# A fused layer norm, state-space and gated feed-forward kernel: the first transposed tile split over two PSUM banks and two copy engines, the second tile in a third bank, end waits sorted

## Chip, cores and metric

The kernel runs on one core of one Trainium2 chip. The metric is device microseconds of one execution on that core. Before the change it took 179.96 us (median of 3 executions, 179.96 to 180.11).

The change touches some half a microsecond of a 180 us kernel.

## The reference

The input x is 2048 rows of 512 numbers in bf16. It is normalised once, and two branches are added to it. Cut to what matters:

```
xn  = layernorm(x)                                     # over the 512 columns
# branch A: a diagonal complex state space with 512 states
h_t = Lam_bar * h_(t-1) + B_bar @ xn_t                 # scan over the 2048 rows
A   = 2 * real(h @ C.T) + xn * Dskip                   # Lam_bar = exp(exp(log_dt) * Lambda)
# branch B: gated feed-forward, 1376 hidden columns
Bf  = (gelu(xn @ w_gate) * (xn @ w_up)) @ w_down
out = x + A + Bf
```

## The kernel before

The rows are worked in four blocks of 512, each of four tiles of 128 rows. The kernel's matmuls take the normalised x with its 512 columns on the partitions, so each tile is transposed. In the first block TensorE does that: four transposes of 128x128 write one PSUM bank, and one engine copies the bank to SBUF.

```
def TR0(j, eng):                       # tile j of the first block
    if not TBANK:
        TBANK.extend([next_bank(), next_bank()])
    bank = TBANK[j % 2]
    ...
    PE(f, ...)                         # four transposes, one instruction group, into this bank
    dst = XNT[0].ap[:, :, 128 * j:128 * (j + 1)]
    src = pt[:, 0:512].rearrange("p (q t) -> p q t", q=KD)
    if eng == "A":
        GATE["evTA"] = ACT(lambda e: e.activation(dst, src, ACTF.Copy), ...)     # ScalarE copies
    else:
        GATE["evT"] = V(lambda e: e.tensor_copy(dst, src), ...)                  # VectorE copies
```

The start of the program, with what TensorE does in this order:

```
PE(fwarm, ...)                         # 11 matmuls on constants, the warm-up
LN(0, [0, 1], True)                    # layer norm of tiles 0 and 1
TR0(0, "V")                            # tile 0: transposes, VectorE copies
TR0(1, "A")                            # tile 1: transposes, ScalarE copies
fill(2)                                # two more matmuls on constants
LN(0, [2, 3], True, [GATE["evT"]])     # tiles 2, 3: statistics only after a VectorE copy
load_B()                               # more loads: the second and third batch of x, B, weights
GU_first(range(5), range(3))           # gate and up projections of the first block
...
```

The first 12 matmuls in `GU_first` are gate projections of tile 0 (three column groups of 128, four matmuls each). The next 12 are up-projections of tile 0 and need the first chunk of `w_up`, a load issued at the start:

```
for u in range(2):                     # 0: gate, 1: up
    for ft in early:                   # three column groups
        mm(ft, u, 0, 1)                # 4 matmuls, tile 0 only
params()                               # one transpose of parameters, and small VectorE/GpSimd work
for ft in early:
    for u in range(2):
        mm(ft, u, 1, 2)                # tile 1
late = [ft for ft in fts if ft not in early]
mm(late[0], 0, 0, 2)
TR0(2, "V")                            # tiles 2 and 3
TR0(3, "A")
...
```

TensorE and the load queue keep the order of the program text, but VectorE, ScalarE and GpSimd are ordered by a list scheduler in the kernel, from estimated durations. So an edit of the first microseconds can reorder VectorE anywhere. And the layer norms of later blocks compute the square root of the variance as a power on GpSimd (line L609 below; VectorE then takes the reciprocal).

```
def SKIP(b):
    ...
        V(lambda e, ...: e.tensor_tensor(XD[tt].ap, xs.ap, DSKB.ap, ALU.mult), ...)      # L621
```

At the very end the queue that issues the stores waits for every output store:

```
final_waits = [(op.sem, 16) for op in self.out_ops]
```

Of the kernel before, what the change touches and what calls it, by code (L numbers as in the profile page):

```python
# [10 lines left out]
ACTF = mybir.ActivationFunctionType  # L11
BF16, F32, I32 = dt.bfloat16, dt.float32, dt.int32
# [64 lines left out]
class Sched:  # L77
# [205 lines left out]
    def emit(self):  # L283
        nc, es = self.nc, self.es
        order = self.order
        esem = {}
        for e in ENGINES:
            if any(op.kind == "eng" for op in order[e]):
                esem[e] = es.enter_context(nc.semaphore("q_" + e))
        cnt = {e: 0 for e in ENGINES}  # L290
        nd = 0
        for e in ENGINES:
            for op in order[e]:
                if op.kind == "eng":
                    cnt[e] += 1
                    op.sem, op.val = esem[e], cnt[e]
                else:
                    op.sem, op.val = es.enter_context(nc.semaphore("d%d" % nd)), 16
                    nd += 1
        self.n_sems = len(esem) + nd  # L300
        plan = {}
        nwait = 0
        for e in ENGINES:
            seen = {}
            prog = []
            for op in order[e]:
                need = {}
                for d in op.deps:
                    if d.kind == "eng" and d.eng == e and e == "tensor":
                        continue  # L310
                    key = ("e", d.eng) if d.kind == "eng" else ("d", d.id)
                    if seen.get(key, 0) >= d.val:
                        continue
                    if key not in need or need[key].val < d.val:
                        need[key] = d
                for key, d in need.items():
                    seen[key] = d.val
                waits = [(d.sem, d.val) for d in need.values()]
                nwait += len(waits)
                prog.append((waits, op))  # L320
            plan[e] = prog
        self.n_waits = nwait
        final_waits = [(op.sem, 16) for op in self.out_ops]
        block = es.enter_context(nc.Block())

        def body_for(ename):
            prog = plan[ename]

            def body(h):
                for waits, op in prog:  # L330
                    for (s, v) in waits:
                        h.wait_ge(s, v)
                    ins = op.fn(h)
                    ins.then_inc(op.sem, 1 if op.kind == "eng" else 16)
                if ename == "sync":
                    for (s, v) in final_waits:
                        h.wait_ge(s, v)
            return body

        for e in ENGINES:  # L340
            if plan[e] or e == "sync":
                {"tensor": block.tensor, "vector": block.vector, "scalar": block.scalar,
                 "gpsimd": block.gpsimd, "sync": block.sync}[e](body_for(e))
# [3 lines left out]
NT, NB, KD, KP, KF = 16, 4, 4, 4, 11  # L347
# [6 lines left out]
def d_pe(n_list):  # L354
    return sum(n / 2.4 + 2.5 for n in n_list)
# [5 lines left out]
def d_act(n, ptr=0): return 190.0 + 0.833 * n + 90.0 * ptr  # L361
# [3 lines left out]
def build(nc, ins, out):  # L365
    with ExitStack() as es:
# [4 lines left out]
        A = Arena(arena_t, ARENA_BYTES)  # L371
        PS = [E(nc.psum_tensor("PS%d" % i, [128, 512], F32)) for i in range(8)]
        BANK = [Buf("bank%d" % i, "ps", i, i + 1) for i in range(8)]

        def ring(parent, name, n):
            return [A.sub(parent, "%s%d" % (name, i), i) for i in range(n)]
# [11 lines left out]
        XNT = ring(XNT_all, "XNT", NB)  # L388
# [3 lines left out]
        XN = ring(XN_all, "XN", 8)  # L392
        DSKB = A.alloc("DSKB", [D], BF16)
        XD_all = A.alloc("XD", [NT, D], BF16); XD = ring(XD_all, "XD", NT)
        IDN = A.alloc("IDN", [128], BF16)
# [20 lines left out]
        XT0 = XTk[0]  # L416
# [88 lines left out]
        V = lambda fn, dur, r, w, tag="", after=(): S.op("vector", fn, dur, r, w, tag, after)  # L505
        ACT = lambda fn, dur, r, w, tag="", after=(): S.op("scalar", fn, dur, r, w, tag, after)
        POOL = lambda fn, dur, r, w, tag="": S.op("gpsimd", fn, dur, r, w, tag)
        PE = lambda fn, dur, r, w, tag="": S.op("tensor", fn, dur, r, w, tag)
# [14 lines left out]
        def next_bank():  # L523
            b_ = rstate["n"] % 8
            rstate["n"] += 1
            return b_
# [24 lines left out]
        GATE = {"before_gelu": [], "nh": 0}  # L551
# [71 lines left out]

        TBANK = []

        def TR0(j, eng):
            if not TBANK:
                TBANK.extend([next_bank(), next_bank()])
            bank = TBANK[j % 2]
            pt = PS[bank].bitcast(BF16)  # L630

            def f(e):
                ins_ = None
                for q in range(KD):
                    ins_ = e.transpose(pt[:, 128 * q:128 * (q + 1)], XN[j].ap[:, 128 * q:128 * (q + 1)], IDN.ap)  # L635
                return ins_
            PE(f, 56.0 * KD, [XN[j], IDN], [BANK[bank]], "T0")
            dst = XNT[0].ap[:, :, 128 * j:128 * (j + 1)]
            src = pt[:, 0:512].rearrange("p (q t) -> p q t", q=KD)
            if eng == "A":  # L640
                GATE["evTA"] = ACT(lambda e: e.activation(dst, src, ACTF.Copy), d_act(512), [BANK[bank]], [XT0[j]], "evT")
            else:
                GATE["evT"] = V(lambda e: e.tensor_copy(dst, src), 420, [BANK[bank]], [XT0[j]], "evT")  # L643

        def TR(b):
            tts = list(range(4 * b, 4 * b + 4))
# [62 lines left out]
            V(lambda e: e.tensor_tensor(ssb.ap[:, :, 1, :], TB.ap[:, :, 0, :], TA.ap[:, :, 1, :], ALU.subtract),  # L709
              d_dve_tt2x(2048), [TA, TB], [SSc[k3][s][1] for s in range(KP)], "post_im")  # L710

        def GU_first(fts, early):
            banks = [{ft: next_bank() for ft in fts} for h in range(2)]

            def mm(ft, u, j0, j1):
                W, Wc = ((WG, WGc), (WU, WUc))[u]
                h, q0 = j0 // 2, 256 * u + 128 * (j0 % 2)
                bank = banks[h][ft]

                def f(e):  # L720
                    ins_ = None
                    for dk in range(KD):
                        ins_ = e.matmul(PS[bank][:, q0:q0 + 128 * (j1 - j0)], W.ap[:, dk, 128 * ft:128 * (ft + 1)],  # L723
                                        XNT[0].ap[:, dk, 128 * j0:128 * j1], start=(dk == 0), stop=(dk == KD - 1))
                    return ins_
                PE(f, d_pe([128 * (j1 - j0)] * 4), [Wc[wchunk(ft)]] + XT0[j0:j1], [BANK[bank]], "GU0")

            def evac(ft, h, after=()):
                bank, c0 = banks[h][ft], 256 * h
                GATE["nh"] = kk = (GATE["nh"] + 1) % 3  # L730
                GATE["last_gelu"] = ACT(lambda e: e.activation(GG[kk].ap[:, 0:256], PS[bank][:, 0:256], ACTF.Gelu_apprx_tanh),
                                        d_act(256), [BANK[bank]], [GG[kk]], "gelu", after)
                ACT(lambda e: e.activation(UPB[kk].ap[:, 0:256], PS[bank][:, 256:512], ACTF.Copy),
                    d_act(256), [BANK[bank]], [UPB[kk]], "evU")
                V(lambda e: e.tensor_tensor(HTt[0][ft].ap[:, c0:c0 + 256], GG[kk].ap[:, 0:256], UPB[kk].ap[:, 0:256], ALU.mult),
                  d_dve_tt2x(256), [GG[kk], UPB[kk]], [HTt[0][ft]], "hmul")

            for u in range(2):
                for ft in early:
                    mm(ft, u, 0, 1)  # L740
            params()
            for ft in early:
                for u in range(2):
                    mm(ft, u, 1, 2)
            late = [ft for ft in fts if ft not in early]
            mm(late[0], 0, 0, 2)
            TR0(2, "V")
            TR0(3, "A")
            for ft in early:
                evac(ft, 0, [GATE["evTA"]])  # L750
            for ft in late[1:]:
                mm(ft, 0, 0, 2)
            for ft in late:
                mm(ft, 1, 0, 2)
                evac(ft, 0)
            for ft in fts:
                for u in range(2):
                    mm(ft, u, 2, 4)
                evac(ft, 1)
# [123 lines left out]
        def fill(n):  # L883
            def f(e):
                ins_ = None
                for _ in range(n):
                    ins_ = e.matmul(PS[wb][:, 0:128], WRM.ap, WRM.ap, start=True, stop=True)
                return ins_
            PE(f, 60.0 * n, [WRM], [BANK[wb]], "fill")

        PE(fwarm, d_pe([512] * nwarm) * 1.6, [WRM], [BANK[wb]], "warm")
        LN(0, [0, 1], True)
        TR0(0, "V")
        TR0(1, "A")
        fill(2)
        LN(0, [2, 3], True, [GATE["evT"]])
        load_B()
        GU_first(range(5), range(3))
        tables_dve()
        GATE["before_gelu"] = [tables_act([GATE["last_gelu"]])]  # L900
        BU(0)
# [81 lines left out]
```

## Time and profile before

| | before |
|---|---|
| time, median of 3 | 179.96 us |
| profiled execution | 179.44 us, span 177.6 us |
| TensorE busy | 97% of the span |
| chain of waits on TensorE | 95% |

The first two lines of the page, and its part 4, the shares of the chain of waits that ended last. Busy is in us, then the share of the span and the number of instructions; PE is TensorE, DVE is VectorE, ACT is ScalarE, POOL is GpSimd.

```profile
span 177.6 us, 2519 instructions
...
PE 172.8 (97%) x914; PEld 86.6 (49%) x929; DVE 156.5 (88%) x276; ACT 91.9 (52%) x175; POOL 11.0 (6%) x20
...
PE 95%; DVE 2%; DMA 1%; issue 1%; ACT 0%; DVEq 0%; ACTq 0%
```

TensorE, with 97% of the span and 95% of the chain, is the bottleneck. VectorE is busy for 88% of the span, but has 2% of the chain. The chain of waits of the kernel before, in order of time, shows where TensorE is not yet the limit. Columns: start in us, length in us, what.

```profile
5.20 0.42 DVE arena L614
...
5.67 0.41 PE PS L635 x4
6.08 0.02 issue
6.10 0.43 DVE arena L643
6.54 0.14 issue
6.67 1.50 PE PS L723 x24
...
10.16 0.45 PE PS L635 x8
10.61 5.68 PE PS L723 x52
```

L614 is the normalisation of tile 0, L635 the transposes, L643 VectorE's copy, L723 the gate and up matmuls. Up to 6.67 us the chain runs through the load, the layer norm and the copy. After that it is TensorE with steps of 0.05 us between. So the change works on the last 0.57 us before TensorE takes over: the copy and the hand-over after it.

The timeline of the kernel before in that stretch: start, length, engine, line, operation, and in brackets how long the engine had been idle and who released it. Copies, transposes and matmuls of one group are merged into one line.

```profile
6.10 0.42 DVE L643 COPY arena<-PS 128x512 bf16<-128x512 bf16 x1 [0.17 <-PE PS L635]
...
6.43 0.60 ACT L641 ACTIVATE arena<-PS 128x512 bf16<-128x512 bf16 x1 [1.54 <-PE PS L635]
6.63 1.29 DVE L602 BATCH_NORM_STATS2 arena<-arena 128x6 f32<-128x512 bf16 x2
```

VectorE takes 0.42 us for tile 0. ScalarE takes 0.60 us for the same size of tile 1. VectorE begins the statistics of tiles 2 and 3 (L602) at 6.63.

### The profile page before, as it was taken

The numbers are of one execution on the slowest core, as the hardware profiler recorded it, in microseconds if no ns is written. First come the engines' busy times: TensorE is split into PE (matmuls) and PEld (weight loads), VectorE is DVE, ScalarE is ACT, GpSimd is POOL, SyncE is SP. The second block draws the span as 40 slices with busy tenths as digits, with TensorE's granted clock in tenths as the row PEclk, the third lists the DMA queues.
The fourth block names the chain that finished last, engine by engine and source line by source line (L and its number), as shares of the span: only waits on it lengthen the run. The fifth ranks groups of instructions, "written<-read, shape, count | busy, mean of one in ns | idle before, by whom it ended". The sixth has DMA issues, their size and how long they took to land.

```text
span 177.6 us, 2519 instructions
## 1 busy us (share of the span) xinstructions
PE 172.8 (97%) x914; PEld 86.6 (49%) x929; DVE 156.5 (88%) x276; ACT 91.9 (52%) x175; POOL 11.0 (6%) x20
## 2 busy tenths in 40 slices
PE   7899999999999999999999999999999999999994
PEld 2697464444644444444644444444464444444453
DVE  5759997999998999789999999899999999999211
ACT  3289998976766899002577495000677800900000
POOL 3110028000000002400000000000000000000000
PEclk9999999999999999999999999999999999999999
DMA  5999914988045000002024000000001000003011
GB/s 135 332 302 174 316 28 91 200 222 285 0 95 56 0 0 0 2 30 92 0 59 89 0 6 0 30 30 30 30 4 30 0 0 0 0 0 122 30 51 37
DMA packets 26387, 12.90 MB, mean 73 GB/s; under 512 B 17704, under 2 KB 26376, under 8 KB 26376
## 3 DMA queue, kind: packets, MB, share of 16 engines
q1 hardware_dynamic: 25824, 12.36, 28.4%
q10 hardware_dynamic: 552, 0.40, 0.9%
q8 instruction: 7, 0.11, 0.3%
q14 instruction: 4, 0.03, 0.0%
HBM read 6.46 MB, written 2.10 MB: 48 GB/s over the span
## 4 chain that ended last, share of the span: by engine, by line
PE 95%; DVE 2%; DMA 1%; issue 1%; ACT 0%; DVEq 0%; ACTq 0%
PE PS L838 37%; PE PS L798 34%; PE PS L660 15%; PE PS L723 5%; PE PS L772 3%; DMA arena<-in_A_x_dram 1%; DVE arena L602 1%; PE PS L635 0%; DVE arena L643 0%; DVE arena L614 0%; DVE arena L856 0%; DVE arena L603 0%; ACT arena L607 0%; DVE arena L605 0%; DVE arena L610 0%
## 5 line engine op out<-in xcount | busy, mean ns | idle before, releaser
L838 PE MATMUL PS<-arena 128*128 128x512 bf16 (+3 forms) x317 | 65.9, 366 | 0.3
L798 PE MATMUL PS<-arena 128*128 128x512 bf16 x273 | 60.7, 379 | 0.4
L838 PEld LDWEIGHTS PS<-arena 128*128 128x128 bf16 (+1 forms) x323 | 30.8, 98 | 35.2
L813 ACT ACTIVATE arena<-PS 128x512 bf16<-128x512 f32 x35 | 20.9, 599 | 43.4 <-PE PS L798 32.8
L798 PEld LDWEIGHTS PS<-arena 128*128 128x128 bf16 x280 | 27.3, 98 | 32.1
L693 DVE TENSOR_TENSOR_SCAN arena<-arena 128x512 bf16<-128x512 f32 x32 | 38.8, 1252 | 0.0
L660 PE MATMUL PS<-arena 128*128 128x512 bf16 x126 | 28.0, 379 | 0.1
L816 ACT ACTIVATE arena<-PS 128x512 bf16<-128x512 f32 x35 | 20.8, 598 | 5.6 <-PE PS L798 5.4
L856 DVE TENSOR_TENSOR arena<-PS,arena 128x512 bf16<-128x512 f32 (+2 forms) x17 | 10.9, 651 | 10.4 <-PE PS L838 10.4
L660 PEld LDWEIGHTS PS<-arena 128*128 128x128 bf16 x128 | 12.5, 98 | 14.9
L664 ACT ACTIVATE arena<-PS 128x512 bf16<-128x512 f32 x32 | 17.8, 603 | 3.2 <-PE PS L660 3.2
L818 DVE TENSOR_TENSOR arena<-arena 128x512 bf16<-128x512 bf16 x35 | 14.0, 416 | 1.5 <-ACT arena L816 1.2
L830 ACT ACTIVATE PS<-arena 128x512 f32<-128x512 bf16 (+2 forms) x17 | 9.6, 581 | 6.1 <-DVE arena L856 5.5
L602 DVE BATCH_NORM_STATS2 arena<-arena 128x6 f32<-128x512 bf16 x16 | 10.3, 682 | 1.6 <-DMA arena<-in_A_x_dram 1.5
L723 PE MATMUL PS<-arena 128*128 128x256 bf16 (+1 forms) x104 | 9.3, 248 | 0.2 <-DVE arena L643 0.2
L680 DVE TENSOR_TENSOR arena<-arena 128x4096 bf16<-128x4096 bf16 (+1 forms) x5 | 9.3, 1856 | 0.0
L682 DVE TENSOR_TENSOR arena<-arena 128x4096 bf16<-128x4096 bf16 (+1 forms) x5 | 9.3, 1855 | 0.0
L706 DVE TENSOR_TENSOR arena<-arena 128x4096 bf16<-128x4096 bf16 x4 | 9.1, 2284 | 0.0
L705 DVE TENSOR_TENSOR arena<-arena 128x4096 bf16<-128x4096 bf16 x4 | 9.1, 2283 | 0.0
L723 PEld LDWEIGHTS PS<-arena 128*128 128x128 bf16 x104 | 8.1, 98 | 0.9 <-issue 0.3
L614 DVE TENSOR_SCALAR arena<-arena 128x512 bf16<-128x512 bf16 x16 | 5.7, 405 | 0.3
L772 PE MATMUL PS<-arena 128*128 128x192 bf16 x64 | 5.9, 246 | 0.0
(86 smaller groups left out, 107.7 us busy)
## 6 DMA issues: line engine op xcount, KB each, us to landing
out_dram<-arena SPq DMA_DIRECT2D x15, 128.0 KB, 1.7
arena<-in_A_x_dram SPq DMA_DIRECT2D x3, 512.0 KB, 7.2
arena<-in_B_w_down_dram SPq DMA_DIRECT2D x1, 1280.0 KB, 6.9
arena<-in_A_x_dram SPq DMA_DIRECT2D x4, 128.0 KB, 2.9
arena<-in_B_w_gate_dram SPq DMA_DIRECT2D x1, 512.0 KB, 6.1
arena<-in_B_w_up_dram SPq DMA_DIRECT2D x1, 512.0 KB, 7.0
arena<-in_B_w_gate_dram SPq DMA_DIRECT2D x1, 480.0 KB, 4.1
arena<-in_B_w_up_dram SPq DMA_DIRECT2D x1, 480.0 KB, 5.2
```

The source lines that it names most:

```text
L602: V(lambda e, tt=tt: e.bn_stats(ST[tt].ap, X[tt].ap), d_dve_1x(512), [X[tt]], [ST[tt]], "bnst", after)
L660: ins_ = e.matmul(PS[bank][:, :], BBT[c][dk].ap[:, 128 * s:128 * (s + 1)], XNT[b].ap[:, dk, :], start=(dk == 0), stop=(dk == KD - 1))
L664: ACT(lambda e, bank=bank, k3=k3, s=s, c=c: e.activation(SSc[k3][s][c].ap, PS[bank][:, :], ACTF.Copy), d_act(512), [BANK[bank]], [SSc[k3][ ...
L693: V(lambda e, g=g, rb=rb, init=init: e.tensor_tensor_scan(g.ap, rb, g.ap, init, ALU.mult, ALU.add), d_dve_scan(512), [g, PA[RRr]] + ([CARc ...
L723: ins_ = e.matmul(PS[bank][:, q0:q0 + 128 * (j1 - j0)], W.ap[:, dk, 128 * ft:128 * (ft + 1)], XNT[0].ap[:, dk, 128 * j0:128 * j1], start=( ...
L772: ins_ = e.matmul(dst, XNT[b].ap[:, dk, 128 * j:128 * (j + 1)], WGU[:, :, dk, f0:f0 + m], start=(dk == 0), stop=(dk == KD - 1))
L798: ins_ = e.matmul(PS[bank][0:m, c0:c1], W.ap[:, dk, 128 * ft:128 * ft + m], XNT[b].ap[:, dk, c0:c1], start=(dk == 0), stop=(dk == KD - 1))
L813: GATE["last_gelu"] = ACT(lambda e, bg=bg, kk=kk, m=m: e.activation(GG[kk].ap[0:m, :], PS[bg][0:m, :], ACTF.Gelu_apprx_tanh), d_act(512), ...
L816: ACT(lambda e, bu=bu, kk=kk, m=m: e.activation(UPB[kk].ap[0:m, :], PS[bu][0:m, :], ACTF.Copy), d_act(512), [BANK[bu]], [UPB[kk]], "evU")
L818: V(lambda e, kk=kk, m=m, ft=ft, k2=k2: e.tensor_tensor(HTt[k2][ft].ap[0:m, :], GG[kk].ap[0:m, :], UPB[kk].ap[0:m, :], ALU.mult), d_dve_tt ...
L838: ins_ = e.matmul(PS[bank][:, c0:c1], l_[:, 128 * j:128 * (j + 1)], r_[:, c0:c1], start=False, stop=last and n == len(ops) - 1, skip_group ...
L856: V(lambda e: e.tensor_tensor(OUTB[ko].ap[:, c0:c1], PS[bank][:, c0:c1], XD[tt].ap[:, c0:c1], ALU.add), d_dve_1x(c1 - c0), [BANK[bank], XD ...
```

## The change

The intent: tile 0 should reach SBUF earlier when two engines each copy half of it. The halves go to different PSUM banks. Tile 1 then goes to a third bank (one that the gate and up projections use later), so that in the program it waits for no copy of tile 0. VectorE copies it in place of ScalarE. Sorting the end waits by the modelled landing time is to save a little at the end. The two filler matmuls are dropped. The core of the diff:

```diff
-        final_waits = [(op.sem, 16) for op in self.out_ops]
+        final_waits = [(op.sem, 16) for op in sorted(self.out_ops, key=lambda o: o.finish)]
...
-        def TR0(j, eng):
+        def TR0(j, engs, first=None):
...
+            per = KD // len(engs)
+            toks = [XT0[j]] if len(engs) == 1 else [Buf("XT0_%d_%d" % (j, n), ...) for n in range(len(engs))]
+            for n, eng in enumerate(engs):
+                bank = TBANK[(j + n) % 2] if first is None else first
...
+                    for q in range(per):
+                        k = per * n + q
+                        ins_ = e.transpose(pt[:, 128 * q:128 * (q + 1)], XN[j].ap[:, 128 * k:128 * (k + 1)], IDN.ap)
...
+                dst = XNT[0].ap[:, per * n:per * (n + 1), 128 * j:128 * (j + 1)]
...
-        TR0(0, "V")
-        TR0(1, "A")
-        fill(2)
+        TR0(0, "VA")
+        hbanks = [{ft: next_bank() for ft in range(5)} for h in range(2)]
+        TR0(1, "V", hbanks[0][4])
         LN(0, [2, 3], True, [GATE["evT"]])
         load_B()
-        GU_first(range(5), range(3))
+        GU_first(range(5), range(3), hbanks)
```

More of the change, by code (lines that the diff above doesn't have):

```diff
@@ L624, in build, with f @@
         TBANK = []
-        def TR0(j, eng):
+        def TR0(j, engs, first=None):
             if not TBANK:
                 TBANK.extend([next_bank(), next_bank()])
-            bank = TBANK[j % 2]
-            pt = PS[bank].bitcast(BF16)
-            def f(e):
-                ins_ = None
-                for q in range(KD):
-                    ins_ = e.transpose(pt[:, 128 * q:128 * (q + 1)], XN[j].ap[:, 128 * q:128 * (q + 1)], IDN.ap)
-                return ins_
-            PE(f, 56.0 * KD, [XN[j], IDN], [BANK[bank]], "T0")
-            dst = XNT[0].ap[:, :, 128 * j:128 * (j + 1)]
-            src = pt[:, 0:512].rearrange("p (q t) -> p q t", q=KD)
-            if eng == "A":
-                GATE["evTA"] = ACT(lambda e: e.activation(dst, src, ACTF.Copy), d_act(512), [BANK[bank]], [XT0[j]], "evT")
-            else:
-                GATE["evT"] = V(lambda e: e.tensor_copy(dst, src), 420, [BANK[bank]], [XT0[j]], "evT")
+            per = KD // len(engs)
+            toks = [XT0[j]] if len(engs) == 1 else [Buf("XT0_%d_%d" % (j, n), "xt", j + n / len(engs), j + (n + 1) / len(engs))
+                                                    for n in range(len(engs))]
+            for n, eng in enumerate(engs):
+                bank = TBANK[(j + n) % 2] if first is None else first
+                pt = PS[bank].bitcast(BF16)
+                def f(e, n=n, pt=pt):
+                    ins_ = None
+                    for q in range(per):
+                        k = per * n + q
+                        ins_ = e.transpose(pt[:, 128 * q:128 * (q + 1)], XN[j].ap[:, 128 * k:128 * (k + 1)], IDN.ap)
+                    return ins_
+                PE(f, 56.0 * per, [XN[j], IDN], [BANK[bank]], "T0")
+                dst = XNT[0].ap[:, per * n:per * (n + 1), 128 * j:128 * (j + 1)]
+                src = pt[:, 0:128 * per].rearrange("p (q t) -> p q t", q=per)
+                if eng == "A":
+                    GATE["evTA"] = ACT(lambda e, src=src, dst=dst: e.activation(dst, src, ACTF.Copy), d_act(128 * per),
+                                       [BANK[bank]], [toks[n]], "evT")
+                else:
+                    GATE["evT"] = V(lambda e, src=src, dst=dst: e.tensor_copy(dst, src), 110 + 0.6 * 128 * per,
+                                    [BANK[bank]], [toks[n]], "evT")
         def TR(b):
@@ L710, in CHAIN, with GU_first @@
               d_dve_tt2x(2048), [TA, TB], [SSc[k3][s][1] for s in range(KP)], "post_im")
-        def GU_first(fts, early):
-            banks = [{ft: next_bank() for ft in fts} for h in range(2)]
+        def GU_first(fts, early, banks):
             def mm(ft, u, j0, j1):
```

## The prediction

> What bounds the kernel now. On the page of the profile TensorE is busy 97% of the 177.6 us span, and the chain of waits is TensorE for 95%. Its pieces in order of time are matmuls end to end from 6.67 us to 175.4 us; the only gaps are 0.05 us "issue" steps. Granted clock 1.0. So time can only be won before 6.67 us (x load, layer norm, first transposes) or after 175.4 us (last add, store, end waits). Anything in between must stay off TensorE's path.
>
> The head, from the timeline: tile 0's four transposes start at 5.67 and end near 6.07; VectorE's copy runs 6.107 to 6.531 (424 ns); the first gate matmul starts at 6.677, about 0.145 us later. That wait of TensorE is 0.17 us, and two filler matmuls lie inside it, so taking them away frees nothing.
>
> What the change does there. Tile 0 goes out in two halves.
> - VectorE, 128x256, may start after two transposes (about 6.0). No row has this shape; from 424 ns at 512 and 164 ns at 12 elements per partition I estimate 290 ns, so done at about 6.29.
> - ScalarE's half still needs all four transposes, so it starts at about 6.107, where the old copy started. Its other 128x256 PSUM copies take 380 to 410 ns: done at 6.49 to 6.51.
> The first matmul now waits for both, so for ScalarE: 6.50 instead of 6.53. Gain 0.02 to 0.05 us. [...] this saves only the difference between 424 ns and ScalarE's slower half.
>
> The next limit is near: the first up-projection chunk lands at 7.145, used at 7.29; 0.04 us earlier still fits.
>
> What it moves. Tile 1's copy goes from ScalarE (597 ns) to VectorE (424 ns, to about 6.85), and tile 2/3's statistics wait for it: 6.63 becomes about 6.95. Their normalised tiles come 0.32 us later, 9.62 and 9.94 instead of 9.29 and 9.61; TensorE wants them at 9.97 and 10.2. No stall, margin about 0.3 us.
>
> The end waits: the built programs' semaphore waits at the end are in identical order in both, so this part is a no-op. The tail in the trace (last store issued 175.72, landed 177.165, end 177.6) stays.
>
> The scheduler also reorders VectorE and slightly ScalarE all through the kernel; TensorE's order is unchanged apart from the fillers. Slacks in the trace: 1.9 us (second state projection's transposed input), about 2 us (last states before the last down-projection), about 0.5 us for a PSUM bank near 31.5 us, freed by ScalarE behind a VectorE multiply that waits for a 2.18 us GpSimd power. I expect them to hold, so the middle neither gains nor loses.
>
> Predicted: 179.92 us (before 179.96), range 179.5 to 180.4. Chances: faster by over 2% 0.005, within 2% 0.98, slower 0.015.
>
> Right if: the first gate matmul starts at 6.62 to 6.66, released by ScalarE; its wait grows to about 0.26 us (fillers gone); the chain is still 95% TensorE; span 177.4 to 177.7; the tail is unchanged.
> Wrong if: TensorE idles at 10 us (tiles 2/3 late) or near 31 us; or its clock falls after the fillers go. [...]

Two passages are cut. One was about two engines at two PSUM banks, the other about the clock after idle time and the cost of losing it; no trace or run of this case shows what they said. No term of the sum is gone: 179.92 us is 179.96 less 0.04, from the gain of 0.02 to 0.05 us in the head. What the cuts take is the reason for expecting a clock of 1.0. That expectation and the one that the two halves run side by side stand as the author's guesses, tested below.

## The result, and the profile after

Ratios here and below are the mean time of one kernel's fast runs over that of the other's of the same rounds, so not quite the ratio of the medians that are quoted.

| | before | after |
|---|---|---|
| time, median of 6 | 179.94 us (179.44 to 180.11) | 179.44 us (179.38 to 179.79) |
| ratio | | 0.9983, interval 0.9967 to 0.9999 |
| profiled execution | 179.44 us | 179.39 us |
| TensorE busy | 97% | 98% |

The interval just misses 1, the median fell by 0.5 us, and 179.44 lies 0.06 below the range that I had given. The ratio times 179.96 is 179.65, which lies inside it. I had predicted 0.04 us. The two profiled executions differ by 0.05 us, the medians by ten times that. Which of the two is the change?

The page and the chain of the kernel after, lines as above. L640 is now the transposes, L649 and L646 are the copies of VectorE and ScalarE, and L729 is the gate and up matmuls.

```profile
span 177.6 us, 2527 instructions
...
PE 173.4 (98%) x927; PEld 86.5 (49%) x927; DVE 156.9 (88%) x277; ACT 91.0 (51%) x175; POOL 9.5 (5%) x20
...
PE 95%; DVE 1%; DMA 1%; ACT 0%; issue 0%; DVEq 0%; ACTq 0%
```

```profile
5.19 0.42 DVE arena L614
...
5.66 0.41 PE PS L640 x4
6.07 0.02 issue
6.09 0.39 ACT arena L646
6.49 0.14 issue
6.62 1.50 PE PS L729 x24
...
10.12 0.45 PE PS L640 x8
10.56 5.68 PE PS L729 x52
```

The step L643 of 0.43 us has become L646 of 0.39 us on another engine. Everything behind it has the same lengths, 0.05 us earlier. (TensorE's busy time rose by 0.6 us, although two fillers went. But the page of the kernel before lists 914 matmuls to 929 weight loads, and that of the kernel after 927 to 927. So 15 matmul records seem to be missing from the first, if each has one load there too, and a difference of this size in busy time says nothing. The chain does not depend on it.)

The timeline of the kernel after in the same stretch:

```profile
5.98 0.86 DVE L649 COPY arena<-PS 128x256 bf16<-128x256 bf16 x2
6.09 0.38 ACT L646 ACTIVATE arena<-PS 128x256 bf16<-128x256 bf16 x1 [1.22 <-PE PS L640]
...
6.95 1.29 DVE L602 BATCH_NORM_STATS2 arena<-arena 128x6 f32<-128x512 bf16 x2
```

The first line merges two copies of VectorE; their records are 5.98 for 292 ns (half of tile 0) and 6.42 for 425 ns (tile 1). VectorE's half is out at 6.28. ScalarE's needs the last two transposes and is out at 6.48. The gate matmuls wait for ScalarE. Tile 2's statistics begin 0.32 us later than before.

### The profile page after: what moved, and what is told of

Same layout as the page of the kernel before. It is cut to its first block, busy times and chain, and to the rows that moved or that the text cites. A ratio compares the mean times of both kernels' runs of the same rounds, so it can differ in the third digit from the quotient of the medians.

```text
span 177.6 us, 2527 instructions
## 1 busy us (share of the span) xinstructions
PE 173.4 (98%) x927; PEld 86.5 (49%) x927; DVE 156.9 (88%) x277; ACT 91.0 (51%) x175; POOL 9.5 (5%) x20
## 4 chain that ended last, share of the span: by engine, by line
PE 95%; DVE 1%; DMA 1%; ACT 0%; issue 0%; DVEq 0%; ACTq 0%
PE PS L844 37%; PE PS L804 34%; PE PS L667 16%; PE PS L729 5%; PE PS L778 3%; DMA arena<-in_A_x_dram 1%; DVE arena L602 1%; PE PS L640 0%; DVE arena L614 0%; ACT arena L646 0%; DVE arena L862 0%; DVE arena L603 0%; ACT arena L607 0%; DVE arena L605 0%; DVE arena L610 0%
## 5 line engine op out<-in xcount | busy, mean ns | idle before, releaser
L804 PE MATMUL PS<-arena 128*128 128x512 bf16 x280 | 61.7, 379 | 0.0
L667 PE MATMUL PS<-arena 128*128 128x512 bf16 x128 | 28.3, 379 | 0.0
L824 DVE TENSOR_TENSOR arena<-arena 128x512 bf16<-128x512 bf16 x35 | 13.7, 417 | 2.7 <-ACT arena L822 2.6
L729 PE MATMUL PS<-arena 128*128 128x256 bf16 (+1 forms) x104 | 9.3, 248 | 0.2 <-ACT arena L646 0.2
L729 PEld LDWEIGHTS PS<-arena 128*128 128x128 bf16 x104 | 8.1, 98 | 1.0 <-issue 0.4
L621 DVE TENSOR_TENSOR arena<-arena 128x512 bf16<-128x512 bf16 x16 | 6.1, 416 | 0.0
```

The costliest lines, as they stand in the source:

```text
L667: ins_ = e.matmul(PS[bank][:, :], BBT[c][dk].ap[:, 128 * s:128 * (s + 1)], XNT[b].ap[:, dk, :], start=(dk == 0), stop=(dk == KD - 1))
L729: ins_ = e.matmul(PS[bank][:, q0:q0 + 128 * (j1 - j0)], W.ap[:, dk, 128 * ft:128 * (ft + 1)], XNT[0].ap[:, dk, 128 * j0:128 * j1], start=( ...
L804: ins_ = e.matmul(PS[bank][0:m, c0:c1], W.ap[:, dk, 128 * ft:128 * ft + m], XNT[b].ap[:, dk, c0:c1], start=(dk == 0), stop=(dk == KD - 1))
L824: V(lambda e, kk=kk, m=m, ft=ft, k2=k2: e.tensor_tensor(HTt[k2][ft].ap[0:m, :], GG[kk].ap[0:m, :], UPB[kk].ap[0:m, :], ALU.mult), d_dve_tt ...
```

## Two things a trace of one execution gives here

I read three events from the records of every profiled execution: the start of the first gate matmul (number 1), the start of the first up matmul (number 13 of L729), and the landing of the first chunk of `w_up`. Behind number 13, TensorE runs 167.80 us to the start of its last matmul, plus whatever stalls there are. The table is in us from the start of the span (all its times lie 2 to 5 ns above those that `prof` prints, which changes no difference by more than that).

| kernel | profiled, us | gate matmul 1 | `w_up` chunk landed | matmul 13 | 13th to the last |
|---|---|---|---|---|---|
| before | 179.44 | 6.677 | 7.145 | 7.344 | 167.80 |
| after | 179.39 | 6.628 | 7.038 | 7.295 | 167.80 |
| after_again | 180.13 | 6.649 | 7.955 | 8.001 | 167.81 |
| sort_only | 180.67 | 6.701 | 7.481 | 7.527 | 168.85 |
| swap | 179.80 | 6.817 | 7.212 | 7.484 | 168.04 |
| split_only | 179.71 | 6.738 | 7.558 | 7.604 | 167.81 |
| tile1_only | 179.47 | 6.712 | 7.029 | 7.379 | 167.80 |
| best | 179.70 | 6.857 | 7.550 | 7.595 | 167.81 |
| fill_back | 179.61 | 6.850 | 7.215 | 7.517 | 167.80 |
| reorder | 179.85 | 6.756 | 7.703 | 7.749 | 167.81 |
| best_reorder | 179.43 | 6.512 | 7.278 | 7.324 | 167.81 |
| before_late | 180.82 | 6.661 | 7.410 | 7.456 | 169.07 |
| after_late | 180.76 | 6.946 | 7.244 | 7.613 | 168.83 |
| late_reorder | 180.63 | 6.914 | 7.107 | 7.580 | 168.72 |

Two rules fit all 14 rows.

1. Number 13 starts at the later of (number 1 plus 0.667 us, for 12 matmuls) and (the landing plus 0.046 us). In 7 of the 14 the landing is the later one: after_again, sort_only, split_only, best, reorder, best_reorder and before_late.
2. The time of the execution is the start of number 13 plus 172.10 us (within 0.03 us), plus the stalls behind it, which are the last column less 167.80. For after: 7.295 + 172.10 = 179.395, measured 179.39. For after_again: 8.001 + 172.10 = 180.10, measured 180.13.

So one program differs between two executions because the head varies, and here by the landing of one load. The same kernel after took 179.39 with the chunk at 7.04 and 180.13 with the chunk at 7.96. Its chain of waits in the later execution, and TensorE's timeline:

```profile
2.65 5.30 DMA arena<-in_B_w_up_dram
...
8.00 0.84 PE PS L729 x12
```

```profile
6.65 0.83 PE L729 MATMUL PS<-arena 128*128 128x128 bf16 x12 [0.24 <-ACT arena L646]
8.00 0.84 PE L729 MATMUL PS<-arena 128*128 128x128 bf16 x12 [0.52 <-DMA arena<-in_B_w_up_dram]
```

TensorE does its 12 gate matmuls, then idles for 0.52 us until the chunk is there (0.52 counts from the modelled end of the twelfth; by rule 1 number 13 could have started at 7.316 = 6.649 + 0.667, so 0.685 us earlier). The chain then goes through the load, and the copies of tile 0 are not on it at all. In such an execution the change cannot save anything.

## The experiments

All kernels were correct. Each is compared with runs of the kernel before on the same chip; they ran in three sessions: sort_only, after_again, swap and split_only; before_late, after_late, best and fill_back; reorder, late_reorder, best_reorder and tile1_only. I held four explanations of the 0.3 us (0.17%) against each other: the split really gains 0.3 us; another part of the change does; a reordering far from the head does; it is scatter.

### 1. What is scatter: sort_only and after_again

sort_only is the kernel before with the sorted end waits alone. The program built from it turned out to be the same instruction for instruction: stores land in issue order in the scheduler's model, so sorting changes nothing. It is therefore a second copy of the kernel before.

```diff
-        final_waits = [(op.sem, 16) for op in self.out_ops]
+        final_waits = [(op.sem, 16) for op in sorted(self.out_ops, key=lambda o: o.finish)]
```

> Only the end waits are sorted. My theory: the built program is instruction for instruction that of before, so ratio 1.000 (interval within 0.997 to 1.003), first gate matmul at 6.67 to 6.68 us, released by VectorE, and the last waits at the same times (176.1 to 177.25 us). It is also the control of how far two timings of one program lie apart on this chip. Rival (the end waits in order of landing give part of the 0.3 us): ratio near 0.998 to 0.999 and an earlier end after the last landing.

after_again is the kernel after, unchanged.

> The changed kernel once more. Theory A (only the 0.05 us of the head are real, the rest of the 0.3 us in the means is scatter between executions): ratio 0.9990 to 1.0005 with an interval that holds 0.9997. Rival B (there is a further gain of about 0.25 us somewhere in most executions of before, which its one profile at 179.44 us did not catch): ratio again 0.997 to 0.999, interval below 0.9997; and a profile of before that took about 179.95 us would show the missing time as a wait that the changed kernel does not have.

Measured: before 179.62 (11 executions, 179.45 to 180.63); sort_only 179.49 (179.45 to 180.67), ratio 1.0000 (0.9974 to 1.0026); after_again 179.57 (179.49 to 180.13), ratio 0.9998 (0.9977 to 1.0019). The 0.17% did not come back, though the second interval is too wide to exclude it. The identical program reached 180.67 once, a whole microsecond over its median. The lowest times of all sessions lie 0.05 us apart, as the gain in the head would have it: 179.43 in 39 executions of the kernel before, 179.38 in 12 of the kernel after. Executions of 180.0 us or more came in 6 of the 39 and in 2 of the 12. So the first 0.3 us was most probably scatter between executions; the times alone do not prove it. The sorted end waits are a no-op, as predicted.

The 180.67 execution of sort_only happened to be the profiled one, and shows a second source of scatter. Its chain of waits, in pieces up to the stall:

```profile
17.29 6.68 DMA arena<-in_A_x_dram
...
28.39 2.19 POOL arena L609
...
33.67 0.50 ACT arena L816
...
34.22 1.89 PE PS L660 x8
```

The third batch of x landed at 23.97, against 23.01 in the kernel before's profile. From there a chain runs through layer norm, a GpSimd power of 2.19 us, VectorE, and ScalarE's copies (L816) to TensorE. 1.05 us were lost near 31 to 34 us. This is the chain that I had named in the prediction with a slack of "about 0.5 us". Experiments 4 and 5 go after it.

### 2. What the head gains and what sets it: swap, split_only, tile1_only, fill_back

The change has three parts in the head. I took them one at a time. One limit of these tests: each edit of the head also lets the list scheduler reorder VectorE and ScalarE elsewhere (fill_back alone keeps the order of the kernel after), so the whole times compare more than the part that is named.

swap: ScalarE, the slower copier, gets the half that is ready first.

```diff
-        TR0(0, "VA")
+        TR0(0, "AV")
```

> The changed kernel, but ScalarE copies the first half of tile 0 and VectorE the second. My theory (the slower copy sets the start, and it started last): ScalarE 5.99 to 6.375, VectorE 6.10 to 6.39, first gate matmul at about 6.53 instead of 6.63, so 0.10 us earlier. The up-projection's first chunk landed at 7.04 to 7.15 and is then wanted at about 7.14, so up to 0.05 us may be lost to it again: span 0.05 to 0.10 us shorter than the changed kernel's, ratio to before about 0.9991 (theory A) or about 0.9975 (rival B). Rival (bank or write contention makes the concurrent copies slower): one of the two copies takes well over 292 or 384 ns and the start does not move.

split_only: tile 1 stays with ScalarE, as in the kernel before.

```diff
-        TR0(1, "V", hbanks[0][4])
+        TR0(1, "A", hbanks[0][4])
```

> Tile 0 split as in the change, but tile 1 stays with ScalarE (third bank, after its half of tile 0). My theory: first gate matmul again at 6.62 to 6.64 us; ScalarE copies tile 1 from 6.48 to 7.08; VectorE is free at 6.28, so the statistics of tiles 2 and 3 start as soon as their gate opens, near 6.4 us instead of 6.95; but TensorE does not need them before 9.95, so the time is that of the changed kernel within 0.03 us. Rival (the earlier or later statistics matter for the time): a gain or loss of 0.2 us or more against the changed kernel.

tile1_only: tile 0 whole with VectorE, as before, tile 1 on VectorE and in the third bank.

```diff
-        TR0(0, "VA")
+        TR0(0, "V")
```

> Only the second part of the change: tile 0 goes whole through VectorE as before, tile 1 through VectorE from the third bank, fillers out. My theory: start of tile 0's copy to first gate matmul 0.57 us as before; statistics of tiles 2 and 3 begin at about 7.0 us and delay their transposes by 0 to 0.1 us near 10 us; ratio to before 0.999 to 1.001. Rival (moving tile 1 is what helps): the start as early as in the changed kernel.

fill_back: the kernel after, with the two fillers.

```diff
         TR0(1, "V", hbanks[0][4])
+        fill(2)
```

> The changed kernel with the two filler matmuls put back after tile 1's transposes; all other engines as in the change. My theory (they lay inside the wait for the copy): the first gate matmul starts at the same distance from the start of ScalarE's copy (0.53 us), ratio to before within 0.001 of the changed kernel's. Rival (they keep the clock up): without them the clock would fall or rise later; then fill_back would be faster by 0.1 us or more.

| kernel | median, us (lowest to highest) | ratio (interval) | later copy of tile 0, its start to gate matmul 1, us |
|---|---|---|---|
| before | in each session 179.62 to 179.65 | | 0.57 |
| after_again | 179.57 (179.49 to 180.13) | 0.9998 (0.9977 to 1.0019) | 0.53 |
| swap | 179.70 (179.61 to 179.80) | 0.9997 (0.9979 to 1.0015) | 0.44 |
| split_only | 179.70 (179.53 to 179.84) | 0.9995 (0.9974 to 1.0015) | 0.53 |
| fill_back | 179.57 (179.36 to 179.83) | 0.9992 (0.9976 to 1.0007) | 0.53 |
| tile1_only | 179.55 (179.47 to 179.75) | 0.9993 (0.9982 to 1.0005) | 0.57 |

No time differs from that of the kernel before by more than scatter. The last column does tell the parts apart. It is read from the records, and does not depend on when the transposes began or on how far apart they started. The split alone is worth 0.04 us (0.57 to 0.53): it is the same with and without the move of tile 1, and with and without fillers. Giving ScalarE the early half would be worth a further 0.09 us: VectorE's half, the later one, takes 292 ns and not 384.

The obvious rival, that the two copies slow each other down, falls. In the kernel after, the two overlap from 6.10 to 6.28. VectorE's copy takes 292 ns and ScalarE's 384, and in swap each of them takes the same within 1 ns. Both pairs overlap, so the better check is fill_back: there the overlap is only 0.09 us, and the copies take 292 and 384 ns again. So no slowing shows at these sizes, with the halves in two banks. Both halves in one bank were not tried.

The profiled execution of swap gained nothing from its shorter copy, and lost 0.23 us more. One line of its TensorE timeline and one piece of its chain:

```profile
5.73 1.03 PE L640 MATMUL PS<-arena 128*128 128x128 bf16 x8
```

```profile
10.30 0.68 PE PS L640 x8
```

Eight transposes took 1.03 us, where the kernel after took 0.72. They start 0.11 us apart, not 0.056. At the other end, the transposes of tiles 2 and 3 took 0.68 us, where they took 0.45: TensorE waited there, because the normalised tiles 2 and 3 came late. VectorE copies tile 1 in swap, and the slow transposes made it begin the statistics at 7.33, 0.38 us later than in the kernel after. Matmul 13 was itself 0.19 us later, so by these numbers 0.19 of the margin was gone, which alone would still have fitted (an estimate). fill_back, also with slow transposes (five of the eight) and with VectorE on tile 1, had no wait. The rest is swap's own order on ScalarE. The scheduler had put a gelu (L739) ahead of the square root of these tiles (L607), whose input was ready at 9.04. Two lines of its timeline:

```profile
9.01 0.38 ACT L739 ACTIVATE arena<-PS 128x256 bf16<-128x256 f32 x1 [2.47 <-PE PS L729]
...
9.29 0.20 ACT L607 ACTIVATE arena<-arena 128x2 bf16<-128x2 bf16 x1
```

The square root began 0.42 us after the VectorE instruction ahead of it (L605) had begun, against 0.21 in fill_back, so the gelu cost 0.21 us, nearly the whole loss. The margin that I had called "about 0.3 us" was used up by the two together. Neither was tested alone.

The slow transposes are not peculiar to swap. TensorE's spacing has a step early in every profile. In the heads of before and after, the warm-up matmuls (512 columns) start 427 ns apart until about 4.0 us, and 216 ns apart after that. Transposes (128 columns) start 107 ns apart ahead of the step and 56 ns behind it. In late_reorder the step came a little earlier, between 3.5 and 3.9 us. In split_only, fill_back, best and swap it came after the warm-up had ended: the first three, five, seven and all eight of the eight transposes still were at the slow spacing of 107 ns, so until 5.9 us in the first and past 6.4 us in the last (the eight took 0.73, 0.84, 0.91 and 1.03 us, in the kernel after 0.72). (In after_again, sort_only and after_late it fell between the last warm-up matmul and the transposes, in the others within the warm-up.) All 14 issue the same warm-up from 0.99 us on. So the step came between 2.5 and 2.9 us after the first warm-up matmul in late_reorder, and over 5.4 us after it in swap. I took it for a rise of TensorE's clock, but that is not shown: the granted clock in the profile is 1.00 from the start to 8 us in before, after, best and swap alike. I read the step from the spacing alone.

Were the dropped fillers to blame? fill_back has them, and its step was late. The kernels before and after, one with and one without, both had the early step. And the fillers come behind the transposes (in fill_back at 6.34 us, the transposes from 5.67), so they can't change the spacing of these. What sets the step in a given execution stays open.

### 3. Both halves of the best head: best

best combines ScalarE on the early half with ScalarE on tile 1, so VectorE is free for tiles 2 and 3.

```diff
-        TR0(0, "VA")
+        TR0(0, "AV")
...
-        TR0(1, "V", hbanks[0][4])
+        TR0(1, "A", hbanks[0][4])
```

> ScalarE copies the first half of tile 0 and then tile 1, VectorE the second half of tile 0 only, so that neither the start nor the statistics of tiles 2 and 3 wait for the slower copy. My theory: last copy of tile 0 to first gate matmul 0.43 us from its start as in swap (0.53 in the changed kernel, 0.57 before), so the first gate matmul near 6.53 us [...]; statistics near 6.5 us; no wait at 10 us (swap showed one of about 0.2 us there). Against before on the same chip 0.10 to 0.15 us: ratio near 0.9993, inside the scatter. Rival: the wait moves to the first up-projection chunk (landed 7.04 to 7.96 us), and the gain at the first gate matmul is gone by the 13th.

In terms of the spacing, 6.53 us was forecast for executions with the step by 5 us, and up to 0.2 us later for the others (an estimate: four transposes at 107 ns and not 56).

Measured: 179.54 (179.48 to 179.70), ratio 0.9991 (0.9976 to 1.0005). The hand-over is 0.44 us as hoped. Its profiled execution had seven of the eight transposes at the slow spacing (number 1 at 6.857) and the chunk at 7.550, so it shows no gain (row of the table). No stall at tiles 2 and 3.

### 4. The chain at 31 us, with the third batch of x delayed: before_late and after_late

In sort_only a late batch of x cost 1.05 us. The scheduler had ordered VectorE differently in the changed kernel, and the GpSimd power in the middle took 1.01 us there, not 2.18. I asked whether that makes the changed kernel stand lateness better. To make lateness on purpose, both kernels got one more load of 384 KB, into space that a later load fills again, right ahead of that batch. The order of all other instructions stayed the same in each.

```diff
-            ld_x(2)
+            S.dma(lambda e: e.dma_start(X_all.ap[:, 12:15, :], x2[1536:1920, :].rearrange("(j p) d -> p j d", p=128)),
+                  0, writes=X[12:15], tag="ld_dum", issue=0.0)
+            ld_x(2)
```

> The kernel before with one more load of 384 KB (data that is loaded again later) queued ahead of the third batch of x, so that this batch lands about 1.0 to 1.2 us later; every other instruction is that of before, in the same order. Rival B in its sharper form (before has a bank chain near 31 us with about 0.5 us of slack that breaks when this load is late, as in the 180.67 us execution of sort_only, where it landed at 23.97 instead of 23.01 us): 0.4 to 1.0 us slower than before, ratio 1.002 to 1.006, with TensorE waiting for ScalarE between 31 and 34 us. Theory A alone (nothing but the head matters): ratio 1.000, no wait of TensorE after 7 us.

> The changed kernel with the same extra load. If its new VectorE order gives the chain near 31 us more room (GpSimd's power took 1.01 us in both its profiles, 2.18 us in both of before, and the bank was free about 0.5 us earlier): it loses at least 0.3 us less than before_late, so 0 to 0.5 us, ratio to before 0.999 to 1.003. If the order does not matter: it loses as much as before_late, less 0.05 us.

Measured: before_late 180.74 (180.36 to 182.07), ratio 1.0068 (1.0038 to 1.0097); after_late 180.51 (180.10 to 180.87), ratio 1.0045 (1.0028 to 1.0063), both against the undelayed kernel before. In the profiled executions the batch landed at 24.62 and 24.97 (in that of the kernel before at 23.01). The groups of waits of TensorE, before_late first, then after_late:

```profile
PE PS L798 <- ACT arena L781: 1.1, 1, 1.1
```

```profile
PE PS L667 <- DMA arena<-arena: 0.5, 1, 0.5
...
PE PS L804 <- ACT arena L787: 0.2, 1, 0.2
```

In before_late, TensorE loses 1.1 us waiting for ScalarE to empty a PSUM bank. In after_late the same wait (L787 there) costs 0.2 us, but a new one of 0.5 us shows, at the transposed input of the third block (a DMA transpose), which is late for the same reason: the chain of waits runs to it from the landing of the batch, through VectorE's layer norm. So the chain moved to another place and the loss shrank only a little: by the last column of the table from 1.27 to 1.03 us, with a batch that landed 0.35 us later. Both forecasts were missed: before_late lies above its 1.002 to 1.006, after_late above its 0.999 to 1.003. The two intervals overlap, so whether the changed kernel suffers less on the whole is not settled. What is shown is that the wait behind L609 and L781 reaches 1.1 us when x is late.

### 5. What makes the power long: reorder, late_reorder, best_reorder

The power is one GpSimd instruction on 4 elements per partition. The lines of the timeline around it in the kernel before:

```profile
27.43 2.18 POOL L609 TENSOR_TENSOR arena<-arena 128x4 bf16<-128x4 bf16 x1
27.67 1.08 DVE L621 TENSOR_TENSOR arena<-arena 128x512 bf16<-128x512 bf16 x3
...
29.65 0.18 DVE L610 RECIPROCAL arena<-arena 128x4 f32<-128x4 bf16 x1 [0.90 <-POOL arena L609]
...
30.64 0.55 ACT L781 ACTIVATE arena<-PS 128x192 bf16<-128x192 f32 x2
```

And in the kernel after:

```profile
27.50 1.01 POOL L609 TENSOR_TENSOR arena<-arena 128x4 bf16<-128x4 bf16 x1
27.77 0.41 DVE L621 TENSOR_TENSOR arena<-arena 128x512 bf16<-128x512 bf16 x1
28.10 0.15 DVE L541 TENSOR_TENSOR arena<-arena 128x4 f32<-128x4 bf16 x1
...
30.17 0.55 ACT L787 ACTIVATE arena<-PS 128x192 bf16<-128x192 f32 x2
```

In the kernel before the power overlaps a run of three big multiplies (L621), each of which starts before the one ahead has ended, and the run ends at 28.75 (27.67 + 1.08), and it ends 0.86 us after that, at 29.61. VectorE then idles 0.90 us for it. (The power's record begins before the three, but not before the run: two more multiplies, L735 with 256 columns, come straight ahead of them, and the first of these began at 27.26, before the power.) In the kernel after, the scheduler had put a small multiply (L541, 4 columns) between the big ones, and the power took 1.01 us. My theory, a guess from these two traces, was that the unbroken run of multiplies on VectorE holds the power up. The rival was that the power just takes longer or shorter by itself. The test moves only L541, on the finished order, ahead of the big multiplies; everything else keeps its order:

```diff
         S.schedule()
+        q = S.order["vector"]
+        i = next(n for n, o in enumerate(q) if o.tag == "a")
+        q.insert(next(n for n, o in enumerate(q) if o.tag == "skip"), q.pop(i))
```

reorder is the kernel before with this, late_reorder is before_late with it, and best_reorder is best with it.

> The kernel before with one VectorE instruction (a 4-column multiply) moved from behind to ahead of the three back-to-back skip multiplies near 27.7 us; nothing else. In six profiles GpSimd's second power ended 0.86 to 0.88 us after the first break in VectorE's two-input multiplies (29.61 after 28.75 in before, 29.45 after 28.57 in swap). If the power only needs one break to get in: it ends near 28.6 instead of 29.6 us (1.0 to 1.2 us long instead of 2.18) and ScalarE's second 192-wide gelu starts near 29.7 instead of 30.3 us. Time in undisturbed executions as before (ratio 0.997 to 1.000), because TensorE did not wait there. If the power's length comes from something else: still 2.18 us.

> before_late (x batch about 1.1 us late) with the same one instruction moved. If the power's wait for VectorE's back-to-back multiplies is what made before_late lose 1.08 us at 31.5 us: TensorE's wait there falls to 0.2 to 0.6 us and the time to ratio 1.002 to 1.005 (before_late 1.0068). If not: 1.0068 again, within 0.001.

> best (halves swapped between the engines, tile 1 by ScalarE) with the same instruction moved, as a candidate against both kernels. best's profile still had the power at 2.18 us and TensorE's weight loads waiting 0.17 us at 31.4 us. Expected: that wait gone, ratio to before 0.997 to 0.9995 with few executions above 179.8 us; against the changed kernel at most 0.1 to 0.2 us, so probably not told apart from it by time.

The lines of reorder:

```profile
27.49 1.19 POOL L609 TENSOR_TENSOR arena<-arena 128x4 bf16<-128x4 bf16 x1
27.72 0.16 DVE L541 TENSOR_TENSOR arena<-arena 128x4 f32<-128x4 bf16 x1
27.80 1.08 DVE L621 TENSOR_TENSOR arena<-arena 128x512 bf16<-128x512 bf16 x3
```

The power took 1.19 us in all three kernels with the move, and 2.18 us in before, sort_only, before_late and best, which lack it. (In the other kernels with another order it took 1.01 to 1.98.) So VectorE's order does set how long the power takes: one small instruction, moved ahead of the last three multiplies, made it 0.99 us shorter. That an unbroken run holds the power up fits ten of the 14 profiles, in which the power ends 0.86 to 0.88 us after such a break or the end of the run (in reorder at 28.67, after the end of the L735 pair at 27.80). What exactly lets the power end is not settled. L541 is itself a multiply of two tiles, only a short one (0.16 us, the big ones 0.41). And in the kernel after, and in after_again, fill_back and after_late with the same VectorE order, L541 does not fit as the cause: the power took 1.01 us and ended 0.26 us after L541 did, 0.90 us after the first of the two 256-column multiplies. Why it ended there is open.

The forecast that ScalarE's second gelu of 192 columns would start near 29.7 us failed as a clock time (30.22 in reorder, 30.30 in before), because matmul 13 was 0.41 us later in this execution. Counted from matmul 13 the gelu came 0.49 us earlier, where 0.6 us was forecast.

What the time says is smaller. Undisturbed: reorder 179.85 (179.54 to 179.98), ratio 1.0004 (0.9992 to 1.0016), so nothing gained where the chain has slack (0.997 to 1.000 was forecast). With the late batch: late_reorder 180.63 (180.00 to 180.82), ratio 1.0047 (1.0032 to 1.0061), by which the mean lies where after_late's does, below before_late's 1.0068, with overlapping intervals, and from another session. In its profile the stalls behind matmul 13 sum to 0.92 us (1.27 in before_late), and the wait of 1.1 us has become

```profile
PE PS L660 <- ACT arena L816: 0.4, 1, 0.4
...
PE PS L798 <- ACT arena L781: 0.2, 1, 0.2
```

best_reorder: 179.61 (179.43 to 179.83), ratio 0.9998 (0.9985 to 1.0011); the forecast was 0.997 to 0.9995. The wait of 0.17 us at 31.4 is gone, as forecast. Its profiled execution had the step in the spacing within the warm-up, and is the cleanest look at the best head. TensorE's first gate matmul starts at 6.51, and then comes the load. The timeline of its copies, of the gate matmuls, and of the first weight load for the up matmuls:

```profile
5.96 1.03 ACT L646 ACTIVATE arena<-PS 128x256 bf16<-128x256 bf16 x2 [1.10 <-PE PS L640]
6.07 0.29 DVE L649 COPY arena<-PS 128x256 bf16<-128x256 bf16 x1 [0.17 <-PE PS L640]
...
7.32 0.34 PEld L729 LDWEIGHTS PS<-arena 128*128 128x128 bf16 x6 [0.15 <-DMA arena<-in_B_w_up_dram]
```

Number 1 starts 0.165 us ahead of the kernel before's (6.512 against 6.677). Of that, 0.13 us is the hand-over (0.44 against 0.57); the other 0.03 us is that the transposes happened to begin earlier here, at 5.63 against 5.67. Number 13 starts at 7.324, against 7.344: it would have been ready at 7.179 (6.512 + 0.667), but the chunk landed at 7.278. Of 0.165 us, 0.02 are left, and the execution took 179.43 us against 179.44. In this execution the gain was given back to the landing of one load.

No version beat both kernels by more than scatter.

## Why the prediction was right, point by point

- **What bounds the kernel.** Right. TensorE carries 95% of the chain in both profiles, and with no stall behind it the time is the start of matmul 13 plus 172.10 us.
- **The size of the head gain, 0.02 to 0.05 us.** Right. Number 1 started at 6.628, predicted 6.62 to 6.66 and released by ScalarE. The hand-over shrank from 0.57 to 0.53 us. The costs held: VectorE's half took 292 ns (estimated 290), ScalarE's 384 (estimated 380 to 410; its 20 pieces of that size take 377 to 452 in the trace of the kernel before). TensorE's wait was 0.24 us, predicted 0.26.
- **The time.** 179.92 was predicted, and 179.44 measured in the first rounds, then 179.57 in a later session. The change is worth 0.05 us between clean executions (179.44 to 179.39, which are also close to the lowest times that either kernel showed). It was partly luck that my range held: it was 0.9 us wide, and could not tell a gain of 0.04 us from none or from 0.3 us. Only the events in the head test the forecast. What my number missed was not the change but its starting point: 179.96 was a median of three executions of a kernel whose floor is 179.44, and sessions of it gave 179.62 to 179.65. A range taken around a median of three should have had its low end at the floor less the gain, 179.4.
- **"The next limit is near: the first up-projection chunk lands at 7.145 ... 0.04 us earlier still fits."** The mechanism was right and its size too comfortable. I took one execution's landing for the landing. It lay between 7.03 and 7.96 over 14 profiles, and in 7 of them it decided the start of matmul 13. In the kernel after's second profile it cost 0.685 us (8.001 less 7.316).
- **Tiles 2 and 3, margin about 0.3 us.** Right in the kernel after: statistics at 6.95 as predicted, and no stall in its profile. But in swap's profile the margin was used up, by the slow transposes and by a gelu ahead of the square root, and 0.23 us were lost.
- **The clock does not fall when the fillers go.** Right: the granted clock is 1.00 in the kernel after from start to end, and fill_back has the same hand-over of 0.53 us. That the step in TensorE's spacing comes at such different times (2.5 to over 5.4 us after the first warm-up matmul) I had not foreseen.
- **The end waits are a no-op.** Right: sort_only is the same program, and its ratio is 1.0000. The chain in the tail starts its last step, VectorE's add, at 175.35 in the kernel after and 175.40 before, 0.05 us earlier like all the rest.
- **The middle neither gains nor loses.** Right for the time. The slack of 0.5 us near 31 us is real but is spent in some executions: sort_only's profile lost 1.05 us there with the x batch 0.96 us late. I took the 2.18 us power as given, where the order on VectorE makes it.

What stays open: why the chunk's landing and the x batch's vary, how often the latter is late, and what sets the step in TensorE's spacing. Issuing the `w_up` chunk earlier was not tried. By the rules above it could be worth up to 0.145 us with best_reorder's head (7.324 less 7.179), an estimate from one execution.

## What to carry to other kernels

When two engines share a copy on the critical path, the gain is set by the half that becomes ready last and the engine that has it, so give the early half to the slower engine (here the hand-over was 0.44 us so, and 0.53 us the other way round). Before costing a gain of 0.05 us, find the next limit behind it in several executions and not in one: here a weight load landing some time within 0.9 us was the limit in half of them, and in the cleanest profile of the best head it took 0.145 of 0.165 us. For a sum that small, compare events within a trace (from the copy to the matmul), since the time of an execution carries scatter of 0.3 us that one and the same program shows as well (medians of the kernel before: 179.94 and 179.62 us in two sessions).
